# Decay totals of the chunks from the ninth on: a small DMA in place of one-column matmuls, with a new order

## The chip, the cores and the metric

The kernel runs on one core of a Trainium2 chip. The metric is the device time of one execution in microseconds; lower is better. Instructions stand in one queue for each engine (PE for matmuls, DVE, ACT, POOL), and SP issues the DMAs; each queue is worked off strictly in order, and engines wait for one another by semaphores.

## The reference

There are two layers, one after the other. The first is a linear attention with a state and a decay for each channel (batch 4, 8 heads, 768 tokens, 48 channels a head):

```python
for t in range(S):
    cur = np.einsum('bhd,bhe->bhde', u[None] * kt, vt)
    y[:, :, t] = np.einsum('bhd,bhde->bhe', rt, state + cur)
    state = wt[:, :, :, None] * state + np.einsum('bhd,bhe->bhde', kt, vt)
```

The second takes y as 3072 tokens of 384 features: `h = x @ w_in` (384 to 2048), `g = s * relu(h)**2 + b`, `out = g @ w_out` (2048 to 384). Inputs and output are fp32.

## The kernel before

**Chunks.** The attention is done in 24 chunks of 128 tokens of one batch row, all 8 heads at once, 384 columns. Chunks 0 to 3 are in pairs ("packed") and follow a way of their own. From chunk 8 on, chunk n and chunk n+4 belong to the same batch row, one after the other; the chunks 20 to 23 are the last of each row and leave no state. Two chunks of attention give one MLP tile of 256 tokens; there are 12 tiles.

**One chunk from 8 on.** ACT takes the logarithm of w (`ln`, L317). PE forms running sums of it over the chunk's tokens with a triangular matrix (`cum`, L391), and four more matmuls with a single column of ones give the total over all 128 tokens, with two heads' channels on the partitions (L397), in four extra columns of the same PSUM tile. ACT takes the exponential of the sums and of the totals in one instruction (`exp`, L413) into `E[:, 0]`; the total's exponential, `lam`, is the decay over the whole chunk. DVE forms the inclusive sum (`inc`, L418) and ACT its negative exponential into `E[:, 1]` (`exn`, L428). DVE multiplies r and k by both halves of E in one instruction (`mul`, L444) into `prd`. There are two buffers of E, used in turn by the chunks.

**State.** POOL spreads `lam` to `l2` (L458). PE forms the chunk's addition to the state (`dmm`, L638), DVE adds the old state (`sup`, L679), and POOL scales the sum by `l2` (`st`, L688). The new state is used by chunk n+4.

**Output of a chunk.** `prd` is transposed, on PE with a copy by ACT for chunks up to 8 (`tr` L471, `tev` L494), by a DMA transpose from chunk 9 on (L501). PE forms the token by token products (`mt`, L543), DVE masks them (`msk`, L555), PE sums over tokens and adds what the state gives (`ymm`, L597 and L606). POOL makes the part with u (`rkp` L322, `rku` L328, `yd` L351), with a reduction on DVE (`cd`, L345); DVE adds it (`yev`, L651), PE transposes and ACT copies to the tile's `xT` (`xtr` L699, `xev` L714).

**MLP tile.** Eight groups of six matmuls with w_in (`g1`, L749), each followed by relu on ACT (L762) and a square on ACT (L772) or DVE (L774); then eight groups of four matmuls with w_out (`g2`, L793), DVE's evacuation (`oev`, L804) and the store (L823). The weights come in four pieces each (`li`, `lo`, L719 and L729), cast by `ci` and `co`.

**Order.** The order is written out by hand in one text, ORDER, of some 1,300 words such as `exp8.0`, and each engine's queue holds its own words in that order; a letter after @ chooses the engine (A, D, P). A number with a plus sign puts in that many matmuls on zeros, to keep PE going at the start. The figures in `add(...)` were a planner's and have no effect on the order that is written out; the buffers' counts (`E=2`, `l2=5`) are real. The core of the part to be changed is

```python
nc.scalar.activation(out=c["E"][:, x, 0:w], in_=ps[:, 0:w], func=AF.Exp)
...
in1=c["E"][:, :, 0:HD].rearrange("t x (h d) -> t x h d", h=H),
```

Of the kernel before, what the change touches and what calls it, by code (L numbers as in the profile page):

```python
# [8 lines left out]
FP32 = mybir.dt.float32  # L9
# [15 lines left out]
PK = 4  # L25
PKD = 1.55
# [12 lines left out]
load0.0 ln0 load0.2 load0.1 ln1 +17 cum0.0 cum0.1 exp0.0 mul0.0 cum1.0 cum1.1 exp0.1 exp1.0 mul0.1  # L39
+3 tr0 load0.3 l21 exp1.1 mul1.0 mul1.1 vb0@A l20 vb1@A load_u u_mm rkp0 tr1 dmm0 u_ev load2.0  # L40
load4.0 tev0 tev1 sup0 ln2 rku0 load2.1 st0 cd0 rkp1 ln3 +5 mt0 +1 cum2.0 cum2.1 load2.3 load2.2
msk0.0 li0 cum3.0 ln4 vb3@A msk1.0 exp2.0 vb2@A msk0.1 li2 +1 cum4.0 exp3.0 msk1.1 yd0 mul2.0 cum3.1
rku1 exp2.1 exp3.1 mul2.1 cd1 l22 mul3.0 ymm0 ci0@A ymm1 li1 yev0 exp4.0 tr2 dmm1 yd1 mul3.1 +8 xtr0
rkp3 li3 tev2 yev1 rku3 sup1 xev0 st1 tr3 rkp2 ci2@D xtr1 xev1 dmm2 sup2 lo0 tev3 load5.0 +3 g10.0
ci1@A mt2 msk3.0 relu0.0 lo1 g10.1 g10.2 msk2.0 msk2.1 sq0.0@A relu0.1 msk3.1 rku2 ci3@A g10.3 g10.4
st2 relu0.4 relu0.2 l23 l24 ymm3 cd3 sq0.1@D yd3 ymm2 lo2 cd2 lo3 yev3 xtr3 small2 yd2 co0@D g10.5
relu0.3 sq0.2@A sq0.4@A ln5 yev2 relu0.5 g10.6 xtr2 g20.4 xev2 csred0@D xev3 load6.0 load4.1 load4.2
load5.1 sq0.3@A load5.2 relu0.6 cum5.0 g10.7 co1@D sq0.5@A load6.1 csred1@D csadd1@D co2@D g11.0
g20.0 relu0.7 exp5.0 sq0.7@A relu1.0 g11.1 csred2@D cum5.1 exp5.1 sq0.6@A g20.1 g11.2 g11.3 cum4.1
g20.5 co3@D small relu1.3 relu1.2 relu1.1 sq1.0@A load7.0 csadd2@D load6.2 ln6 load4.3 load5.3 g20.6  # L50
g11.4 csred3@D g11.5 relu1.4 g20.2 exp4.1 csadd3@D load6.3 sq1.3@A g20.3 cum6.0 relu1.5 g20.7
cssplit sq1.1@A mul4 csspread sq1.2@D csevac g11.6 exp6.0 relu1.6 cum6.1 mul5 tr4 dmm3 exp6.1 l26
g11.7 tev4 tr5 oev0.1 tev5 sup3 relu1.7 sq1.4@A oev0.0 g21.0 g21.1 rkp4 mt4 rkp5 g21.4 vb4@P mul6
msk5.0 sq1.5@A sq1.7@A rku4 rku5 msk4.0 load8.0 l25 msk4.1 tr6 cd4 dmm4 load9.0 sup4 yd4 load7.1 st4
load7.2 sq1.6@A vb5@A cd5 ln7 vb6@A tev6 load7.3 msk5.1 load8.1 ln8 g21.5 g21.2 g21.6 load8.2 dmm5
cum7.0 exp7.0 yd5 ymm4 g21.7 sup5 yev4 ymm5 cum7.1 xtr4 cum8.0 yev5 inc8 load9.3 load10.0 load9.1
ln9 dmm6 rkp6 st3 l27 exp7.1 load11.0 load8.3 xev4 vb7@P xtr5 xev5 cum9.0 exp8.0 mul7 load9.2 sup6
g21.3 exn8 g12.0 exp9.0 g12.1 rkp7 rku6 relu2.0 tr7 g12.2 relu2.1 inc9 st5 oev1.1 oev1.0 sq2.1@A
rku7 g12.3 dmm7 tev7 relu2.2 sq2.0@D relu2.3 g12.4 sup7 mul8 cd6 rkp8 relu2.4 g12.5 g22.4 mt6
relu2.5 g22.0 msk6.0 sq2.3@A tr8 g12.6 msk7.0 msk6.1 cd7 sq2.2@A sq2.5@A msk7.1 g22.5 ymm6 ln10  # L60
g22.1 yd6 rku8 sq2.4@A yev6 tev8 exn9 cd8 relu2.6 ln11 yd7 vb8@P st7 ymm7 xtr6 g22.6 cum10.0 yev7
xev6 store0.1 load11.1 vb9@A mul9 inc10 xtr7 l29 l28 rkp9 g12.7 load10.1 xev7 cum11.0 g22.2 g13.0
st6 relu2.7 exp10.0 dmm9 sq2.7@D load11.2 g13.1 store0.0 load10.2 exn10 g13.2 exp11.0 inc11 sq2.6@A
relu3.0 sq3.0@A exn11 sup9 relu3.1 mul10 rku9 dmm8 g13.3 sup8 mul11 tev9 g22.7 g13.4 g13.5 load11.3
load10.3 load12.0 load13.0 g22.3 oev2.1 cd9 tev11 load12.1 tev10 oev2.0 relu3.3 relu3.2 st8 rkp10
relu3.4 mt8 l211 yd9 msk8.0 msk8.1 g13.6 sq3.1@A sq3.4@A relu3.5 sq3.3@A l210 yd8 g23.4 rku10 vb10@A
g13.7 relu3.7 vb11@P msk9.0 sq3.2@A rkp11 ymm8 msk9.1 g23.0 ln12 yev8 st9 ymm9 xtr8 relu3.6 g23.1
sq3.6@A sq3.5@D yev9 cum12.0 xev8 xtr9 xev9 inc12 store1.0 ln13 exp12.0 dmm11 g23.5 load12.2 sup11
g23.2 dmm10 cd10 g14.0 sup10 exn12 relu4.0 rku11 load13.3 mt10 g23.6 g14.1 sq3.7@A msk10.0 msk10.1
msk11.0 cum13.0 g14.2 g14.3 store1.1 load13.1 msk11.1 inc13 mul12 cd11 load13.2 load14.0 relu4.1  # L70
ymm10 relu4.2 sq4.0@D exp13.0 rkp12 store2.1 relu4.3 exn13 g23.3 g23.7 yd10 load16.0 load15.0
load14.1 sq4.1@A ymm11 g14.4 load14.3 oev3.1 yd11 rkp13 g24.0 g14.5 st11 rku12 g14.6 load14.2
sq4.2@A sq4.3@A ln14 relu4.4 load15.1 l212 relu4.5 mul13 relu4.6 yev11 load12.3 oev3.0 yev10 rku13
xtr11 g24.4 ln15 sq4.5@A xtr10 cum14.0 vb13@P sq4.4@D g14.7 inc14 xev10 g24.1 g24.5 l213 xev11 cd13
exp14.0 cum15.0 g15.0 exn14 relu4.7 g15.1 load15.2 relu5.0 cd12 inc15 relu5.1 exp15.0 tev12 exn15
sq4.6@A sq5.1@D mul14 sq4.7@D g15.2 g24.2 g24.6 g15.3 l215 ln16 tev13 relu5.3 store2.0 sq5.0@D g15.4
g24.3 vb14@P vb12@A relu5.2 l214 yd12 mul15 cum16.0 dmm13 g15.5 inc16 load17.0 sq5.3@A dmm12
load15.3 tev14 relu5.5 oev4.0 exp16.0 relu5.4 tev15 st10 sq5.2@A g24.7 g25.4 sup13 l216 rkp15 st13
g15.6 sq5.4@A mt12 store3.0 load16.1 yd13 sq5.5@A rku15 store3.1 relu5.6 sup12 oev4.1 ln17 g15.7
msk12.0 load18.0 vb15@A load16.2 g25.5 dmm14 exn16 relu5.7 g25.0 msk13.0 rkp14 msk12.1 cum17.0 ymm12  # L80
msk13.1 exp17.0 sq5.7@A g25.1 ymm13 load17.1 load16.3 yev12 sup14 xtr12 yev13 xev12 load17.2 dmm15
inc17 g25.6 xtr13 rku14 load17.3 st12 sq5.6@A sup15 cd15 g25.2 mt14 load18.1 load19.0 msk14.0
msk15.0 exn17 g25.7 xev13 msk14.1 g16.0 cd14 g16.1 yd15 yd14 g16.2 msk15.1 rkp16 relu6.0 sq6.0@A
relu6.2 relu6.1 ymm14 g16.3 ymm15 yev14 g16.4 xtr14 yev15 relu6.3 sq6.3@A sq6.1@A g16.5 oev5.1 mul16
xtr15 st14 sq6.2@A g16.6 xev14 g26.4 l217 g25.3 g16.7 tev16 relu6.4 load18.2 rkp17 xev15 vb16@P
relu6.5 g17.0 g26.5 relu6.6 relu6.7 sq6.5@A rku16 st15 vb17@P rku17 mul17 sq6.4@D oev5.0 ln18 g17.1
dmm16 relu7.1 cum18.0 sq6.6@D sq6.7@A inc18 sup16 cd17 relu7.0 sq7.0@D g17.2 tev17 cd16 relu7.2
load18.3 store4.0 load20.0 store4.1 load19.1 exp18.0 ln19 g26.0 g26.1 g17.3 dmm17 g26.2 g17.4
cum19.0 yd17 load21.0 l218 vb18@P load19.2 yd16 load20.1 st16 exn18 sq7.1@A relu7.3 g26.6 sup17
inc19 relu7.4 sq7.3@A exp19.0 sq7.4@A mt16 g17.5 msk16.0 msk17.0 msk17.1 g17.6 g26.3 g26.7 ln20  # L90
relu7.5 msk16.1 ymm17 exn19 sq7.5@A oev6.1 sq7.2@A g17.7 relu7.6 relu7.7 yev17 sq7.6@A ymm16 g27.4
load19.3 store5.1 l219 rkp18 ln21 g27.5 rku18 load22.0 load20.2 cum20.0 xtr17 yev16 xtr16 oev6.0
# [71 lines left out]
def kernel(  # L164
# [72 lines left out]
    NBX = 4  # L237
    PRD_B = 4
    MB = 4
    NLW = 3  # L240
    logws = [
        const.tile([128, H, 64], BF16, name=f"logw{i}", tag=f"logw{i}")
        for i in range(NLW)
# [916 lines left out]
```

## Time and profile before

| what | us |
|---|---|
| median of three runs | 184.68 (184.1 to 184.84) |
| the profiled execution | 184.8 |
| its span, first to last instruction | 183.0 |
| PE busy | 176.2 |
| ACT busy | 145.4 |
| DVE busy | 143.9 |
| POOL busy | 104.4 |
| one product L444, mean of 20 | 1.228 |
| one activation L413 / L428, mean | 0.498 / 0.529 |
| one one-column matmul L397, mean of 64 | 0.164 |

The profile's page gives busy time by engine, then the span in 40 slices of 4.6 us with the busy tenths of each engine, then the chain of work that ended last, then groups of instructions with the idle time of the engine before them. Means of groups on PE are latencies of pipelined matmuls: two that follow one another start closer than the mean says. Line numbers are those of the kernel before.

### The profile page before, as it was taken

To read this page: it belongs to the slowest core of one execution; us is meant where nothing else is said; L and a number is where in the kernel's file an instruction comes from. 1 tells how busy PE (TensorE), PEld (TensorE's weight loads), DVE (VectorE), ACT (ScalarE), POOL (GpSimd) and SP (SyncE) were. 2 spreads that over 40 slices of the span, in tenths; PEclk is the share of its full clock that TensorE was granted. 3 is DMA by queue.
4 is the path that set the end of the run, shared out by engine and by line. 5 is a ranking of instruction groups with operands and counts; after the bars stand their busy time and mean duration, and the time that the engine had idled before them with its cause. 6 is when DMAs were issued, how large, how long until landed. Compare 5 with 4: busy or idle time off the path is not lost.

```text
span 183.0 us, 5106 instructions
## 1 busy us (share of the span) xinstructions
PE 176.2 (96%) x1994; PEld 139.8 (76%) x1994; DVE 143.9 (79%) x251; ACT 145.4 (79%) x285; POOL 104.4 (57%) x139
## 2 busy tenths in 40 slices
PE   7999699999999999999999999999999999999992
PEld 5568588777798798687887798877876798788871
DVE  7587599999999989899589889768779897670432
ACT  3875999999999998969899869997897395685530
POOL 3695950008997869828478769778508694130000
PEclk9999999999999999999999999999999999999999
DMA  5999999979979689998999973999599919810112
GB/s 153 313 277 337 386 387 358 179 144 212 201 150 230 137 171 147 235 217 163 211 201 178 231 154 61 197 206 225 106 207 197 223 23 161 217 61 31 43 43 86
DMA packets 113449, 34.14 MB, mean 187 GB/s; under 512 B 108177, under 2 KB 111378, under 8 KB 113426
## 3 DMA queue, kind: packets, MB, share of 16 engines
q1 hardware_dynamic: 113426, 33.83, 81.2%
q8 instruction: 15, 0.25, 0.5%
q14 instruction: 8, 0.07, 0.1%
HBM read 25.17 MB, written 4.72 MB: 163 GB/s over the span
## 4 chain that ended last, share of the span: by engine, by line
PE 83%; SPq 6%; DMA 5%; DVE 2%; ACT 1%; issue 1%; DVEq 0%
PE o_ps L793 34%; PE h_ps L749 33%; DMA wi_st<-in_moe_w_in_dram 5%; SPq L304 4%; PE mt_ps L543 3%; PE y_ps L606 2%; PE xt_ps L699 2%; PE cums L391 2%; PE y_ps L597 2%; PE d_ps L638 2%; SPq L719 1%; PE trps L471 1%; DVE prd L444 1%; ACT w_in L870 1%; PE y_ps L586 1%
## 5 line engine op out<-in xcount | busy, mean ns | idle before, releaser
L749 PE MATMUL h_ps<-xT,w_in 128*128 128x256 bf16 x576 | 72.9, 273 | 1.5 <-ACT xT L714 1.3
L793 PE MATMUL o_ps<-w_out,gT 128*128 128x384 bf16 (+1 forms) x400 | 73.0, 319 | 0.1
L762 ACT ACTIVATE rh<-h_ps 128x512 bf16<-128x512 f32 x96 | 54.8, 601 | 14.8 <-PE h_ps L749 14.2
L749 PEld LDWEIGHTS <-w_in 128*128 128x128 bf16 x576 | 61.2, 114 | 5.9 <-issue 1.4
L793 PEld LDWEIGHTS <-gT 128*128 128x128 bf16 x400 | 36.5, 98 | 17.1 <-issue 0.2
L772 ACT ACTIVATE gT<-rh 128x512 bf16<-128x512 bf16 x68 | 41.4, 639 | 0.3
L351 POOL TENSOR_TENSOR yd<-vt,cd 128x384 bf16<-128x384 f32 x20 | 17.7, 887 | 24.0 <-DVE cd L345 17.4
L555 DVE TENSOR_TENSOR mt_sb<-mt_ps,tri_strict 128x512 bf16<-128x512 f32 x40 | 25.0, 681 | 2.3 <-PE mt_ps L543 2.2
L328 POOL TENSOR_TENSOR rku<-rkp,u_bc 128x384 f32<-128x384 f32 x24 | 25.4, 1064 | 0.6
L774 DVE TENSOR_TENSOR gT<-rh 128x512 bf16<-128x512 bf16 x28 | 15.7, 574 | 12.4 <-ACT rh L762 12.3
L444 DVE TENSOR_TENSOR prd<-rkt,E 128x768 bf16<-128x768 f32 x20 | 24.5, 1228 | 0.0
L322 POOL TENSOR_TENSOR rkp<-rkt 128x384 f32<-128x384 f32 x20 | 21.1, 1058 | 1.9 <-DMA rkt<-in_k_dram 1.9
L413 ACT ACTIVATE E<-cums 128x388 f32<-128x388 f32 (+1 forms) x32 | 15.6, 498 | 3.6 <-PE cums L391 1.9
L804 DVE SCALAR_TENSOR_TENSOR o_sb<-o_ps,s_bc,bconst 128x384 f32<-128x384 f32 (+1 forms) x25 | 14.7, 594 | 4.5 <-PE o_ps L793 4.4
L688 POOL TENSOR_TENSOR st<-stmp,l 128x384 bf16<-128x384 bf16 x16 | 17.1, 1072 | 1.8 <-DVE stmp L679 1.8
L458 POOL TENSOR_TENSOR l<-E,par 128x8 f32<-128x8 f32 x20 | 6.5, 330 | 20.2 <-ACT E L413 20.2
L651 DVE TENSOR_TENSOR x_sb<-y_ps,yd 128x384 bf16<-128x384 f32 x24 | 13.3, 553 | 3.9 <-PE y_ps L606 3.1
L714 ACT COPY xT<-xt_ps 128x384 bf16<-128x384 bf16 x24 | 11.0, 487 | 3.1 <-PE xt_ps L699 3.1
L345 DVE TENSOR_REDUCE cd<-rku 128x8 f32<-128x384 f32 x24 | 13.0, 544 | 0.2
L418 DVE TENSOR_TENSOR inc<-cums,logw 128x384 f32<-128x384 f32 x16 | 8.8, 552 | 3.9 <-PE cums L397 1.4
L317 ACT ACTIVATE logw<-wt 128x384 bf16<-128x384 f32 x20 | 10.6, 529 | 0.0
L679 DVE TENSOR_TENSOR stmp<-d_ps,st 128x384 bf16<-128x384 f32 x16 | 8.7, 549 | 1.5 <-PE d_ps L638 1.3
(93 smaller groups left out, 202.0 us busy)
## 6 DMA issues: line engine op xcount, KB each, us to landing
out_dram<-o_sb SPq DMA_DIRECT2D x23, 192.0 KB, 3.1
wt<-in_w_dram SPq DMA_DIRECT2D x20, 192.0 KB, 3.9
rkt<-in_r_dram SPq DMA_DIRECT2D x20, 192.0 KB, 3.9
rkt<-in_k_dram SPq DMA_DIRECT2D x20, 192.0 KB, 4.0
vt<-in_v_dram SPq DMA_DIRECT2D x20, 192.0 KB, 3.8
wi_st<-in_moe_w_in_dram SPq DMA_DIRECT2D x4, 768.0 KB, 7.4
wo_st<-in_moe_w_out_dram SPq DMA_DIRECT2D x4, 768.0 KB, 7.0
pkt<-in_w_dram SPq DMA_DIRECT2D x2, 384.0 KB, 3.7
```

The lines of the kernel that those rows point to most:

```text
L322: nc.gpsimd.tensor_tensor(out=rkp, in0=c["r"], in1=c["k"], op=ALU.mult)
L328: nc.gpsimd.tensor_tensor(out=rku.rearrange("t h d -> t (h d)"), in0=c["rkp"].rearrange("t h d -> t (h d)"), in1=u_bc, op=ALU.mult,)
L351: nc.gpsimd.tensor_tensor(out=yd, in0=c["v"], in1=c["cd"].unsqueeze(2).to_broadcast([128, H, D]), op=ALU.mult,)
L413: nc.scalar.activation(out=c["E"][:, x, 0:w], in_=ps[:, 0:w], func=AF.Exp)
L444: nc.vector.tensor_tensor(out=prd[:, :, :, 0:D], in0=c["rk"], in1=c["E"][:, :, 0:HD].rearrange("t x (h d) -> t x h d", h=H), op=ALU.mult,)
L555: nc.vector.tensor_tensor(out=c["mt"][:, sg], in0=c["mt_ps"][sg], in1=(masks[:, n % 2] if packed(n) else tri_strict) .unsqueeze(1) .to_bro ...
L688: nc.gpsimd.tensor_tensor(out=c["st_new"], in0=c["stmp"].rearrange("q p (g e) -> q p g e", g=2), in1=c["l2"].unsqueeze(3).to_broadcast([12 ...
L749: nc.tensor.matmul(ps[:, f, :], lhsT=w_in_sb[ft // FPP][:, kt, :].rearrange("p (m j) -> p j m", j=FPP)[:, ft % FPP, :], rhs=xT[T][:, kt, : ...
L762: nc.scalar.activation(out=rh, in_=hs[T, i], func=AF.Relu)
L772: nc.scalar.activation(out=g, in_=rh, func=AF.Square)
L774: nc.vector.tensor_tensor(out=g, in0=rh, in1=rh, op=ALU.mult)
L793: nc.tensor.matmul(os_[T, k][:, cols], lhsT=gT[T][:, ft, tt * 128 : (tt + 1) * 128], rhs=w_out_sb[ft // FPP][:, ft % FPP, cols], start=(ft ...
```

## The change

From chunk 8 on (`LAM = 8`), PE no longer forms the total. The negative exponential of the inclusive sum at the chunk's last token, row 127 of `E[:, 1]`, is 1 over the same decay. Two DMAs (`lam`, by SP) carry this one row to the partitions of the state, one for the even and one for the odd heads, 48 partitions of 4 values each, into a ring of six small tiles. DVE then takes the reciprocal of 128x4 and spreads it to `l2` (128x8), which POOL did before. Chunks 20 to 23 need no total and had none.

So that the row can be carried, E of these chunks is stored with the channel outside and the head inside ("d h" in place of "h d"). Both activations write it so, and the product reads it so: neighbours along the inner loop of 48 lie 8 words apart. Buffer E is released by the product and by the two DMAs, in place of POOL's L458. `dmm` and `sup` no longer wait for `l2`.

The copies `tev` and `xev` can now be put on ACT or DVE, and the whole ORDER is another one: over all, 6 copies `xev` and 3 `tev` are on DVE, 23 squares in place of 28, and the first pieces of w_in are asked for earlier. The matmuls on zeros at the start are 21 of 512 columns, where they were 38 of 256.

```diff
--- before.py
+++ after.py
@@ constants @@
 PK = 4
+LAM = 8
...
 ORDER = """
-load0.0 ln0 load0.2 load0.1 ln1 +17 cum0.0 cum0.1 exp0.0 mul0.0 cum1.0 cum1.1 exp0.1 exp1.0 mul0.1
-+3 tr0 load0.3 l21 exp1.1 mul1.0 mul1.1 vb0@A l20 vb1@A load_u u_mm rkp0 tr1 dmm0 u_ev load2.0
...
+load0.0 load_u ln0 load0.1 load0.2 +6 u_mm ln1 load2.0 cum0.0 cum0.1 exp0.0 load0.3 exp0.1 cum1.0
+cum1.1 exp1.0 mul0.0 mul0.1 exp1.1 ln2 mul1.0 +1 tr0 mul1.1 u_ev ln3 l21 +2 tr1 li0 tev0@D cum2.0
...
+load9.2 g21.7 load11.0 dmm6 xev5@D load10.1 lam8 rkp6 tr7 oev1.0 store0.1 dmm7 g12.0 sup6 oev1.1
...
+lam10 tev10 lam11 g13.7 msk8.1 msk9.1 ymm8 oev2.0 vb10@A cd9 relu3.6 cum12.0 exp12.0 rku10 ymm9 yd9
...
 """
@@ -238,6 +240,7 @@
     PRD_B = 4
     MB = 4
     NLW = 3
+    lams = const.tile([128, 6, 8], FP32, name="rlam", tag="rlam")
     logws = [
         const.tile([128, H, 64], BF16, name=f"logw{i}", tag=f"logw{i}")
         for i in range(NLW)
@@ -392,7 +395,7 @@
             ps[:, 0:HD], lhsT=tri_strict if x == 0 else ntri_incl,
             rhs=lw[:, :, 0:D], start=True, stop=True,
         )
-        if x == 0 and cc < NCH - 1:
+        if x == 0 and cc < NCH - 1 and not row_lam(n):
             for p in range(HP):
                 nc.tensor.matmul(
                     ps[:, HD + p : HD + p + 1],
@@ -402,6 +405,12 @@
                     stop=(p == HP - 1),
                 )
 
+    def by_head(ap, n):
+
+        if row_lam(n):
+            return ap.rearrange("t (d h) -> t h d", h=H)
+        return ap.rearrange("t (h d) -> t h d", h=H)
+
     def expo(n, x):
         c = cb[n]
         cc, _ = coords(n)
@@ -409,8 +418,12 @@
         if x == 0:
             E = work.tile([128, 2, HD + 16], FP32, name="E", tag="E", bufs=2)
             c["E"], c["lam"] = E, E[:, 0, HD : HD + HP]
-        w = HD + HP if x == 0 and cc < NCH - 1 else HD
-        nc.scalar.activation(out=c["E"][:, x, 0:w], in_=ps[:, 0:w], func=AF.Exp)
+        w = HD + HP if x == 0 and cc < NCH - 1 and not row_lam(n) else HD
+        if row_lam(n):
+            out, in_ = by_head(c["E"][:, x, 0:HD], n), by_head(ps[:, 0:HD], 0)
+        else:
+            out, in_ = c["E"][:, x, 0:w], ps[:, 0:w]
+        nc.scalar.activation(out=out, in_=in_, func=AF.Exp)
 
     def incl(n):
         c = cb[n]
@@ -426,7 +439,7 @@
     def expn(n):
         c = cb[n]
         nc.scalar.activation(
-            out=c["E"][:, 1, 0:HD], in_=c["inc"], func=AF.Exp, scale=-1.0
+            out=by_head(c["E"][:, 1, 0:HD], n), in_=by_head(c["inc"], 0), func=AF.Exp, scale=-1.0
         )
 
     def mult(n, x=None):
@@ -444,9 +457,22 @@
         nc.vector.tensor_tensor(
             out=prd[:, :, :, 0:D],
             in0=c["rk"],
-            in1=c["E"][:, :, 0:HD].rearrange("t x (h d) -> t x h d", h=H),
+            in1=c["E"][:, :, 0:HD].rearrange(
+                "t x (d h) -> t x h d" if row_lam(n) else "t x (h d) -> t x h d", h=H
+            ),
             op=ALU.mult,
         )
+
+    def row_lam(n):
+        return n >= LAM
+
+    def lamrow(n):
+        c = cb[n]
+        t = lams[:, n % 6]
+        row = c["E"][127:128, 1, 0:HD].rearrange("o (d p g) -> o d p g", g=2, p=HP)
+        for g in range(2):
+            nc.sync.dma_start(out=t[64 * g : 64 * g + D, 0:HP], in_=row[:, :, :, g])
+        c["rlam"] = t
 
     def lam2(n):
         c = cb[n]
@@ -455,6 +481,17 @@
             return
         l2 = work.tile([128, 32], FP32, name="l2", tag="l2", bufs=5)[:, 0 : 2 * HP]
         l2 = l2.rearrange("q (p g) -> q p g", g=2)
+        if row_lam(n):
+            t = c["rlam"]
+            nc.vector.reciprocal(out=t[:, HP : 2 * HP], in_=t[:, 0:HP])
+            nc.vector.tensor_tensor(
+                out=l2,
+                in0=t[:, HP : 2 * HP].unsqueeze(2).to_broadcast([128, HP, 2]),
+                in1=par.unsqueeze(1).to_broadcast([128, HP, 2]),
+                op=ALU.mult,
+            )
+            c["l2"] = l2
+            return
         nc.gpsimd.tensor_tensor(
             out=l2,
             in0=c["lam"].unsqueeze(2).to_broadcast([128, HP, 2]),
@@ -480,6 +517,12 @@
                 )
         c["trps"] = ps
 
+    def move(name, out, in_):
+        if pl.ops[name]["eng"] == "ACT":
+            nc.scalar.copy(out=out, in_=in_)
+        else:
+            nc.vector.tensor_copy(out=out, in_=in_)
+
     def tevac(n):
         c = cb[n]
         if packed(n):
@@ -488,10 +531,10 @@
                 pair["RK2"] = work.tile(
                     [128, 2, 2 * HP, 128], BF16, name="RK2", tag="RK2", bufs=1
                 )
-            nc.scalar.copy(out=pair["RK2"][:, n % 2], in_=c["trps"])
+            move(("tev", n), pair["RK2"][:, n % 2], c["trps"])
             return
         RK = work.tile([128, 2 * HP, 128], BF16, name="RK", tag="RK", bufs=RKB)
-        nc.scalar.copy(out=RK, in_=c["trps"])
+        move(("tev", n), RK, c["trps"])
         c["RT"] = RK[:, 0:HP, :]
         c["KT"] = RK[:, HP : 2 * HP, :]
 
@@ -666,8 +709,8 @@
             [128, HP, 2 * D], BF16, name=f"st{bb}", tag=f"st{bb}", bufs=2
         )
         new_v = new.rearrange("q p (g e) -> q p g e", g=2)
-        lbc = c["l2"].unsqueeze(3).to_broadcast([128, HP, 2, D])
         if cc == 0:
+            lbc = c["l2"].unsqueeze(3).to_broadcast([128, HP, 2, D])
             nc.vector.tensor_tensor(
                 out=new_v,
                 in0=c["d_ps"].rearrange("q p (g e) -> q p g e", g=2),
@@ -711,7 +754,7 @@
         T, j = divmod(n, CPT)
         if j == 0:
             xT[T] = mlp.tile([128, KT, TOK], BF16, name="xT", tag="xT", bufs=XTB)
-        nc.scalar.copy(out=xT[T][:, :, j * L : (j + 1) * L], in_=c["xt_ps"])
+        move(("xev", n), xT[T][:, :, j * L : (j + 1) * L], c["xt_ps"])
 
 
     def load_win(i):
@@ -858,7 +901,7 @@
     pl = Plan(
         dict(w=WB, rk=8, v=VB, lw=NLW, prd=NPR, E=2, RK=RKB, M=MB, vb=6, yd=6, x=XSB, RK2=1,
              cd=4, rkp=2, rku=2, l2=5, P=6, o=2, gT=3, xT=XTB, rh=4, inc=1,
-             o_sb=4, wst=4, stmp=2)
+             o_sb=4, wst=4, stmp=2, rlam=6)
     )
     add = pl.add
 
@@ -934,11 +977,11 @@
             [("yd", [("yev", n)])], P - 1, port=True)
         for x in range(1 if one else 2):
             add(("cum", n, x), "PE",
-                (0.35 if pk else 0.163) + (0 if x or not keep else 0.21 if pk else 0.105),
+                (0.35 if pk else 0.163) + (0 if x or not keep or row_lam(n) else 0.21 if pk else 0.105),
                 cum, (n, x), every("ln"),
                 [("P", [("exp", n, x)] + ([("inc", n)] if one else []))], P, lat=0.2, slack=SL)
             add(("exp", n, x), "ACT", 0.43, expo, (n, x), [("cum", n, x)],
-                [] if x else [("E", muls(n) + ([("l2", n)] if keep else []))], P - 3,
+                [] if x else [("E", muls(n) + ([("lam" if row_lam(n) else "l2", n)] if keep else []))], P - 3,
                 after=[("exp", n, 0)] if x else [])
         if one:
             add(("inc", n), "DVE", 0.48, incl, (n,), [("cum", n, 0)], [("inc", [("exn", n)])], P - 3)
@@ -983,11 +1026,15 @@
             add(("xev", n), "SP", 1.2, dxtr, (n,), [("yev", n)] + xd, xt,
                 P - 1000, dma=0.85, slack=0.1)
         if keep:
-            add(("l2", n), "POOL", 0.17, lam2, (n,), [("exp", n, 0)],
+            if row_lam(n):
+                add(("lam", n), "SP", 0.9, lamrow, (n,), [("exn", n) if one else ("exp", n, 1)],
+                    [("rlam", [("l2", n)])], P - 2, dma=0.25)
+            add(("l2", n), "DVE" if row_lam(n) else "POOL", 0.2 if row_lam(n) else 0.17, lam2, (n,),
+                [("lam", n)] if row_lam(n) else [("exp", n, 0)],
                 [("l2", [("st", n)])], P - 2, port=True)
-            add(("dmm", n), "PE", 0.36 if pk else 0.16, dmm, (n,), [a for m in b2 for a in muls(m)] + every("vb") + [("l2", n)] + prev,
+            add(("dmm", n), "PE", 0.36 if pk else 0.16, dmm, (n,), [a for m in b2 for a in muls(m)] + every("vb") + ([] if row_lam(n) else [("l2", n)]) + prev,
                 [("P", [("sup", n)])], P - 4, lat=0.2, slack=SL)
-            add(("sup", n), "DVE", 0.48, supd, (n,), [("dmm", n), ("l2", n)] + prev,
+            add(("sup", n), "DVE", 0.48, supd, (n,), [("dmm", n)] + ([] if row_lam(n) and cc else [("l2", n)]) + prev,
                 [("stmp", [("st", n)])] if cc else [], P - 5)
             if cc:
                 add(("st", n), "POOL", 0.8, sscale, (n,), [("sup", n), ("l2", n)]
@@ -1075,7 +1122,7 @@
         add(("co", i), e, t, cast_out, (i,), [("lo", i)], [], 45.0, port=e != "ACT")
 
 
-    warm_sb = const.tile([128, TOK], BF16, name="warm_sb", tag="warm_sb")
+    warm_sb = const.tile([128, 2 * TOK], BF16, name="warm_sb", tag="warm_sb")
     nc.vector.memset(warm_sb, 0.0)
     nc.vector.memset(logws[0], 0.0)
     make_upper_triangular(nc, tri_strict, val=1.0, diag=False)
@@ -1087,6 +1134,7 @@
     nc.vector.memset(par[0:64, 0:1], 1.0)
     nc.vector.memset(par[64:128, 1:2], 1.0)
     nc.vector.memset(prds[0], 0.0)
+    nc.gpsimd.memset(lams, 1.0)
     nc.vector.memset(logws[1], 0.0)
     for i in range(1, NPR):
         nc.vector.memset(prds[i], 0.0)
@@ -1112,7 +1160,7 @@
                 nc.gpsimd.tensor_copy(out=masks[d, i, c : c + 64], in_=src[d, d])
 
 
-    warm_ps = psO.tile([128, TOK], FP32, name="warm_ps", tag="o")
+    warm_ps = psO.tile([128, 2 * TOK], FP32, name="warm_ps", tag="o")
 
     def warm(n):
         for _ in range(n):
```

## The prediction

> **What bounds the kernel now.** I read the busy shares first, then the slices, then the chain:
>
> ```profile
> PE 176.2 (96%) x1994; PEld 139.8 (76%) x1994; DVE 143.9 (79%) x251; ACT 145.4 (79%) x285; POOL 104.4 (57%) x139
> ...
> PE   7999699999999999999999999999999999999992
> ...
> DVE  7587599999999989899589889768779897670432
> ACT  3875999999999998969899869997897395685530
> ...
> PE 83%; SPq 6%; DMA 5%; DVE 2%; ACT 1%; issue 1%; DVEq 0%
> ```
>
> PE is the bound: 96% busy, nines from the sixth slice to the last but one, 83% of the chain (the shares of SP and DMA are the first 24 us). But the rows of DVE and ACT are full of eights and nines, so PE leads by little. How little, a view of busy time by stretches says (stretch, length, then busy us and counts of PE, PEld, DVE, ACT, POOL, then granted clock, DMA share, GB/s):
>
> ```profile
> 56.00:152.00 96.00, 95.63 (x1058) 76.92 (x1057) 82.37 (x133) 82.06 (x169) 68.91 (x84) 1.00 0.89 177
> 24.00:56.00 32.00, 32.00 (x383) 26.05 (x381) 30.53 (x50) 31.11 (x61) 15.66 (x19) 1.00 0.96 227
> ```
>
> The first stretch holds the products L444 of chunks 8 to 23. DVE is free there for 96 - 82.37 = 13.6 us. In the second, DVE is 30.53 / 32 = 95.4% busy and PE never idles; I take 95.4% as what DVE can carry before PE starves, so 91.6 us of the 96, and the stage can take 91.6 - 82.4 = 9.2 us more DVE work. The groups and the PE timeline that the change touches:
>
> ```profile
> L444 DVE TENSOR_TENSOR prd<-rkt,E x20: 945/1178/1799, 40.0 to 150.7; 128x768 bf16<-128x768 f32 x20
> ```
> ```profile
> L444 DVE TENSOR_TENSOR prd<-rkt,E 128x768 bf16<-128x768 f32 x20 | 24.5, 1228 | 0.0
> L413 ACT ACTIVATE E<-cums 128x388 f32<-128x388 f32 (+1 forms) x32 | 15.6, 498 | 3.6 <-PE cums L391 1.9
> L458 POOL TENSOR_TENSOR l<-E,par 128x8 f32<-128x8 f32 x20 | 6.5, 330 | 20.2 <-ACT E L413 20.2
> ```
> ```profile
> 95.31 0.24 PE L397 MATMUL cums<-ones,logw 128*128 128x1 bf16 x4
> 95.41 0.33 PE L638 MATMUL d_ps<-vb,prd 128*128 128x96 bf16 x4
> ```
>
> The first line gives shortest, median and longest ns; the group lines give us in total, mean ns, and idle time before. The last pair shows what four one-column matmuls really take: each lasts 164 ns in its group (0.24 us for the four), but the next work starts 0.10 us after them.
>
> **What the Trainium skill says.** *Vector Engine (DVE) Microarchitecture Reference*, section 5.2 "Measured stream behaviour on trn2": a DVE port streams at full rate only in runs of at least two adjacent 4-byte words. It prices 1.054 ns per column when all is contiguous, 1.73 when one source hops at every element, 2.50 when both sources or the destination alone step 24 words. The trace agrees on the first: the shortest L444 is 945 ns, 768 x 1.054 = 809 plus 136 fixed. No instruction of the kernel before shows the others. *SBUF — State Buffer*, section "Who interferes with whom": a DVE instruction with two SBUF inputs contends with POOL's reads. L444 agrees: its mean of 1228 ns lies 283 above its shortest. *ScalarE: Activation LUTs*, section "What ACT_TABLE_LOAD costs": 186 + 0.833 N ns for an activation without pointer operands, so 506 for 384 columns; L413's mean is 498. *DMA: Bandwidth & Descriptors*, section "Rules for kernel authors": a strided last dimension is moved as one descriptor per element. No run here shows it yet.
>
> **The change part by part.**
>
> 1. *PE.* The decay column goes from 12 chunks (8 to 19), so 12 x 4 = 48 one-column matmuls at 0.10 us a group: -1.2 us of PE. All of it lies on the path while PE is the bound, none of it where another engine is.
>
> 2. *The layout of E.* This is what I count most. From chunk 8 on, E holds d outside and h inside, so both activations (L413, L428) write, and the product L444 reads, one fp32 every 8 words. L444 then has one source that never offers two adjacent words. Lower bound 768 x (1.73 - 1.054) = 0.52 us more each, upper bound 768 x (2.50 - 1.054) = 1.11, estimates from the section named. The section says small steps cost more than large ones; 8 words is small, but only one source steps. I take 0.8. For 16 products: 8.3, **12.8**, 17.8 us.
>
> 3. *Small DVE work added.* 12 reciprocals of 128x4 and 12 products of 128x8. The nearest rows are DVE's 128x2 memset (60 ns, L1086) and POOL's own 128x8 product (199 ns at its shortest, L458). At 0.12 us each: 24 x 0.12 = 2.9 us (1.4 to 4.8). POOL loses 12 x 0.33 = 4.0 us, off the path.
>
> 4. *Work moved between engines by the new order.* In tiles 2 to 9 DVE has 13 squares for 16: -3 x 0.574 = -1.7 us. Two copies of xT (chunks 11, 12) come to DVE: +1.0. Over the run, ACT has 73 squares for 68 (+5 x 0.64), 6 fewer copies of xT (-6 x 0.49), 3 fewer of RK (-3 x 1.02), 4 fewer casts of v (-4 x 0.52) and one more of w_in (+1.5): about -3.4 us. POOL takes 4 casts of v (+4 x 0.69) and one of w_out.
>
> 5. *ACT's strided writes.* No row and no page prices them. At nothing: 0. At double the column time: 0.833 x 384 = 0.32 us more for 32 activations, 10.2 us. With both in the stage ACT is at 82 + 10 = 92 of 96, below the 31.11 / 32 = 97% it carries from 24 to 56 us. So I count 0 on the path, 3 us at worst. A gain is excluded: nothing gets shorter.
>
> 6. *24 DMAs on SP.* The small b_bc load took 0.43 us to issue, so 24 x 0.43 = 10 us in a queue that waits 16.4 us for the product L444 alone (ahead of its transposes L501), with more behind stores. 192 elements each, 4,608 packets on top of 113,426: 4%. Each pair waits for L428 (or L413), and behind it in SP's order stand loads, stores and transposes. The transposes wait for L444, which itself waits for L428, so they lose only the issue. The landing (3.8 us for a transpose, the row of small consumers) stands before three things: the reciprocal on DVE, and behind it all DVE work in order; the scaling L688 on POOL, needed a whole round of four chunks later; and the reuse of E, two buffers, by the activation two chunks on, with the relus behind it on ACT. I take 0 here: in the new order the last two are mostly several us away. At worst, see the second rival.
>
> 7. *The head.* The first w_in piece is issued seventh instead of eleventh, the r, k and v of the second pair later; 38 warm matmuls of 256 columns become 21 of 512. In the trace the PE's last wait before dense work ends at 23.7 us, on a cast of w_in. Earlier weights against later v: I take 0, and 1.5 us either way.
>
> Sum for DVE in the stage: 82.4 + 12.8 + 2.9 - 1.7 + 1.0 = 97.4 us (92.9 to 102.4 with the two ends of part 2). It carries 91.6, so 5.8 us too much, and at 95.4% that takes 5.8 / 0.954 = 6.1 us (1.4 to 11.3). The saving on PE is lost, since PE then waits for masks, x and the squares from DVE. What is late next is PE at the first matmuls of an MLP tile and at the late squares. The profiled execution took 184.8 us for a span of 183.0; 184.8 + 6.1 = 190.9. The median of the three runs is 184.68, so the two stand alike.
>
> **The rivals.**
>
> *The stride is free, or fits into DVE's idle time: faster.* One mechanism: PE stays the bound and keeps the 1.2 us. 184.8 - 1.2 = 183.6, within 182.1 to 185.1 by the head. For it: below 9.2 us of added DVE work nothing should show, and the low end of part 2 with the other terms gives 82.4 + 8.3 + 2.2 = 92.9, only 1.3 over. It decides where the price of one product falls under (9.2 - 2.2) / 16 = 0.44 us. Against it: the section's price starts at 0.52.
>
> *The new transfers become the wait: slower, by another way.* The landing of 3.8 us, held by SP's order, keeps DVE at the reciprocal or ACT at the next E. Twelve transfers; if four come 2 us late on engines with 10% to spare, and PE's own queue of filled PSUM hides half: 4 us, 184.8 - 1.2 + 4 = 187.6. For it: both engines work strictly in order. Against it: in the new order DVE meets its reciprocal 3 to 20 us of PE work after the transfer. The sign would show in DVE idle before the reciprocal, not in longer products.
>
> *The change does not do what it says:* the instruction lists of the two built programs show 48 one-column matmuls and 24 more DMAs where the diff says so, so I leave no chance for it.
>
> **How the numbers follow.** The forecast, DVE over-full, 0.62; the stride hidden, 0.18; the transfers as the wait, 0.20. Half a per cent (0.9 us) is about what a measurement of this kernel can tell from no change. Faster: 0.13 of the second case, 0.01 of the third. Slower: 0.61, 0.01 and 0.17. Same: the rest, 0.07. The forecast alone spans 186.2 to 196.1, and ACT's 3 us could be on top; the range goes down to 184.0, to take in part of the hidden case, and up to 197.0.
>
> **What would show it.** Right: the products of chunks 8 to 23 last about 2.0 us in the mean (1.75 to 2.35), those before 1.2; DVE is at 95% or more from 56 to 152 us; PE shows waits for DVE (masks, x_sb, gT) of several us in sum where it had none. The one-column group has 16 matmuls left of 64. The activations that write E last between 0.50 and 0.82 us. Wrong: products still near 1.2 us, or PE as full as before in the stage. If the products are long and PE is still full, the 95.4% was too low a ceiling.

## The result and the profile after

The changed kernel takes **191.12 us** (median of four runs, 189.65 to 192.55), the kernel before 184.76 us on the same chip (four runs, 184.1 to 185.83). One of the four, 192.55 us, was in the slower state that some executions of any kernel show; such runs are left out of the ratio and of every median below, and the median of the other three is 190.75 us. The ratio is 1.031, 95% interval 1.022 to 1.040: slower, by 6.0 us between the medians. The profiled execution took 190.75 us, its span is 188.7 us.

The page's shares, the slices and the head of the chain, of the kernel after:

```profile
PE 178.4 (95%) x1929; PEld 137.0 (73%) x1929; DVE 156.4 (83%) x277; ACT 153.0 (81%) x278; POOL 112.0 (59%) x133
...
PE   6999798999999999999989999979989999999993
...
DVE  7379689999998999899799989689879897974322
ACT  3486697899989999989968897699699889863840
...
PE 43%; POOL 15%; DMA 11%; SPq 10%; issue 8%; DVE 7%; ACT 4%; POOLq 0%; ACTq 0%; DVEq 0%
```

PE still has 95% of the span, but its share of the chain falls from 83% to 43%. The row of PE has eights and sevens in the middle, where it had nines without a break. No other engine takes the bound over: POOL, DMA, SP, DVE and ACT share what PE lost. By stretches of the kernel after (stretch, length, busy us and counts of PE, PEld, DVE, ACT, POOL, then clock, DMA share, GB/s):

```profile
24.00:56.00 32.00, 30.89 (x377) 24.57 (x366) 30.76 (x48) 29.38 (x54) 18.03 (x22) 1.00 0.98 239
56.00:152.00 96.00, 93.14 (x971) 73.07 (x970) 86.45 (x150) 85.97 (x159) 70.01 (x69) 1.00 0.86 169
```

From 56 to 152 us PE is idle 2.9 us where it was idle 0.4, and from 24 to 56 us 1.1 us where it never idled. DVE is 86.45 / 96 = 90% busy in the later stretch, ACT as well: both fuller than before (82.4 and 82.1), neither full. The groups on the page of the kernel after that answer to those shown of before:

```profile
L457 DVE TENSOR_TENSOR prd<-rkt,E 128x768 bf16<-128x768 f32 x20 | 31.4, 1568 | 2.8 <-DMA rkt<-in_k_dram 1.9
...
L426 ACT ACTIVATE E<-cums 128x384 f32<-128x384 f32 (+1 forms) x32 | 21.8, 692 | 7.4 <-PE cums L383 2.1
...
L441 ACT ACTIVATE E<-inc 128x384 f32<-128x384 f32 x16 | 14.7, 919 | 0.1
```

The four early products and the other early activations are dense and pull the means of L457 and L426 down. The view of the single instructions shows the 16 products of chunks 8 to 23 at 1.66 us in the mean, 1.55 at the shortest (before: 1.25 and 0.945). The activations of these chunks take 0.89 us (L426, before 0.49) and 0.92 us (L441, before 0.53). So in this execution the written half of the layout costs each ACT instruction 0.39 us and the read half each product 0.42 us. The 0.39 stands in every kernel with strided writes below; the strided products of the others last longer, 1.71 to 1.81 us in the mean. The new transfers and the small DVE work, in the views by group and by DMA issue of the kernel after:

```profile
L487 DVE TENSOR_TENSOR l<-rlam,par 128x8 f32<-128x8 f32 x12 | 4.8, 401 | 0.4
L486 DVE RECIPROCAL rlam<-rlam 128x4 f32<-128x4 f32 x12 | 2.0, 166 | 0.0
```
```profile
rlam<-E SPq DMA_DIRECT2D x24, 0.8 KB, 2.6
```
```profile
POOL st L731 <- DVE l L487: 3.5, 2, 2.8
...
ACT E L426 <- DMA rlam<-E: 1.2, 2, 0.7
```

The second fence is the DMA's median from issue to landing, 2.6 us. The third is the view of waits (total us, times, longest): the state's scaling on POOL waits 3.5 us for a total, and an activation on ACT 1.2 us for the buffer that a transfer holds; neither engine is the bound.

### The profile page after: what moved, and what is told of

The parts are those of the page before. It is cut to its first block, busy times and chain, and to the rows that moved or that the text cites. A ratio compares the mean times of both kernels' runs of the same rounds, so it can differ in the third digit from the quotient of the medians.

```text
span 188.7 us, 5017 instructions
## 1 busy us (share of the span) xinstructions
PE 178.4 (95%) x1929; PEld 137.0 (73%) x1929; DVE 156.4 (83%) x277; ACT 153.0 (81%) x278; POOL 112.0 (59%) x133
## 4 chain that ended last, share of the span: by engine, by line
PE 43%; POOL 15%; DMA 11%; SPq 10%; issue 8%; DVE 7%; ACT 4%; POOLq 0%; ACTq 0%; DVEq 0%
PE h_ps L792 18%; PE o_ps L836 18%; SPq L307 4%; POOL rku L331 4%; DMA pkt<-in_v_dram 4%; POOL rkp L325 4%; POOL st L731 4%; DMA rlam<-E 3%; DMA wt<-in_w_dram 2%; DVE mt_sb L598 2%; ACT E L426 2%; DMA vt<-in_v_dram 2%; SPq L299 2%; DVE prd L457 2%; SPq L762 2%
## 5 line engine op out<-in xcount | busy, mean ns | idle before, releaser
L836 PE MATMUL o_ps<-w_out,gT 128*128 128x384 bf16 (+1 forms) x400 | 74.0, 320 | 0.8 <-ACT gT L815 0.6
L815 ACT ACTIVATE gT<-rh 128x512 bf16<-128x512 bf16 x73 | 44.3, 637 | 0.3
L457 DVE TENSOR_TENSOR prd<-rkt,E 128x768 bf16<-128x768 f32 x20 | 31.4, 1568 | 2.8 <-DMA rkt<-in_k_dram 1.9
L331 POOL TENSOR_TENSOR rku<-rkp,u_bc 128x384 f32<-128x384 f32 x24 | 27.6, 1152 | 1.8 <-DVE u_bc L940 1.0
L325 POOL TENSOR_TENSOR rkp<-rkt 128x384 f32<-128x384 f32 x20 | 25.6, 1284 | 4.9 <-DMA rkt<-in_k_dram 4.9
L426 ACT ACTIVATE E<-cums 128x384 f32<-128x384 f32 (+1 forms) x32 | 21.8, 692 | 7.4 <-PE cums L383 2.1
L817 DVE TENSOR_TENSOR gT<-rh 128x512 bf16<-128x512 bf16 x23 | 13.2, 587 | 6.0 <-ACT rh L805 5.9
L915 POOL CAST vb<-vt 128x384 bf16<-128x384 f32 x16 | 12.0, 756 | 5.5 <-DMA vt<-in_v_dram 5.4
L441 ACT ACTIVATE E<-inc 128x384 f32<-128x384 f32 x16 | 14.7, 919 | 0.1
L694 DVE TENSOR_TENSOR x_sb<-y_ps,yd 128x384 bf16<-128x384 f32 x24 | 12.8, 551 | 1.6 <-PE y_ps L649 1.0
L522 ACT COPY xT<-xt_ps 128x384 bf16<-128x384 bf16 x18 | 8.7, 494 | 4.8 <-PE xt_ps L742 4.8
```

What stands on the lines that cost most here:

```text
L325: nc.gpsimd.tensor_tensor(out=rkp, in0=c["r"], in1=c["k"], op=ALU.mult)
L331: nc.gpsimd.tensor_tensor(out=rku.rearrange("t h d -> t (h d)"), in0=c["rkp"].rearrange("t h d -> t (h d)"), in1=u_bc, op=ALU.mult,)
L426: nc.scalar.activation(out=out, in_=in_, func=AF.Exp)
L441: nc.scalar.activation(out=by_head(c["E"][:, 1, 0:HD], n), in_=by_head(c["inc"], 0), func=AF.Exp, scale=-1.0)
L457: nc.vector.tensor_tensor(out=prd[:, :, :, 0:D], in0=c["rk"], in1=c["E"][:, :, 0:HD].rearrange("t x (d h) -> t x h d" if row_lam(n) else " ...
L815: nc.scalar.activation(out=g, in_=rh, func=AF.Square)
```

## The experiments

All times are medians, set against runs of the kernel before on the same chip beside them; "+2.0" means over that. These were 184.32 us for experiments 1 to 4; 184.56 for the first two kernels of experiment 5, for experiment 6 and for the first kernel of experiment 7; 184.12 for the last two of experiment 5; and 185.13 for the last two of experiment 7. In experiments 1 to 3 and in the dense kernels of experiment 5 some products or totals take other channels' decays, as the expectations say; their time is read, not their output.

**1. The layout taken away.** The kernel after, with both activations and the product dense; order, DMAs and reciprocals stay.

```diff
     def by_head(ap, n):
-        if row_lam(n):
-            return ap.rearrange("t (d h) -> t h d", h=H)
         return ap.rearrange("t (h d) -> t h d", h=H)
...
-                "t x (d h) -> t x h d" if row_lam(n) else "t x (h d) -> t x h d", h=H
+                "t x (h d) -> t x h d", h=H
```

> The changed kernel, with E of every chunk stored with heads outside as before: both activations write and the product reads adjacent words. All else (order, DMAs, reciprocals) stays; the DMAs still pick the same addresses, so the decays they carry belong to other channels. Theory 1 (the one-word steps of E cost the time): products near 1.23 us and activations near 0.50 and 0.53 us, time 184 to 186.5 us. Theory 2 (the new order costs it) and theory 3 (waits for the new transfers cost it): 189 to 191 us although the instructions are short again.

Measured: 186.62 us, ratio 1.013 (1.008 to 1.018), +2.3. The stretches of this kernel:

```profile
24.00:56.00 32.00, 31.04 (x366) 24.78 (x365) 30.74 (x48) 29.06 (x55) 18.09 (x21) 1.00 1.00 239
56.00:152.00 96.00, 96.00 (x1032) 77.76 (x1031) 83.98 (x158) 81.96 (x167) 64.72 (x72) 1.00 0.90 180
```

The time lies just above the first range of the expectation. PE has no idle time left from 56 to 152 us; the idle time before 56 us stays. Of the 6.0 us, the layout is what is left, 6.0 - 2.3 = 3.7, and it acts in the stage of the later chunks.

**2 and 3. Each half of the layout alone.** First only ACT writes with steps and the product reads dense; then only the product reads with steps. Each is one of the two edits above undone.

> The changed kernel, but the product reads E as if heads were outside (adjacent words, so it multiplies by the decays of other channels); the activations still write one word in eight. Products 1.23 us, activations 0.89 and 0.92 us. If the cost is DVE's, as the prediction had it: 185 to 187 us. If ACT's longer writes carry it: 188 to 191 us.

> The changed kernel, but the activations write adjacent words and the product reads one word in eight (so it multiplies by the decays of other channels, and the DMAs carry those of other channels). Products 1.55 us at the shortest, activations 0.50 and 0.53. If the cost is DVE's: 188 to 191 us. If it is ACT's: 185 to 187 us.

Measured: ACT's half 188.26 us (ratio 1.019, 1.012 to 1.025), +1.6 over the dense kernel; DVE's half 188.65 us (1.023, 1.018 to 1.029), +2.0 over it. The groups and the later stretch, first of the kernel with ACT's half, then of that with DVE's:

```profile
L457 DVE TENSOR_TENSOR prd<-rkt,E 128x768 bf16<-128x768 f32 x20 | 22.7, 1133 | 3.0 <-ACT E L441 1.7 <-DMA rkt<-in_k_dram 1.2
...
L441 ACT ACTIVATE E<-inc 128x384 f32<-128x384 f32 x16 | 14.8, 923 | 0.0
```
```profile
56.00:152.00 96.00, 95.74 (x1013) 76.63 (x1011) 81.64 (x157) 89.20 (x164) 64.92 (x73) 1.00 0.86 172
```
```profile
L455 DVE TENSOR_TENSOR prd<-rkt,E 128x768 bf16<-128x768 f32 x20 | 33.4, 1671 | 0.6 <-DMA rkt<-in_k_dram 0.3 <-ACT E L424 0.2
...
L439 ACT ACTIVATE E<-inc 128x384 f32<-128x384 f32 x16 | 8.4, 525 | 0.5 <-DVE inc L429 0.4
```
```profile
56.00:152.00 96.00, 95.58 (x1004) 76.06 (x1002) 91.70 (x155) 80.18 (x162) 70.82 (x72) 1.00 0.83 169
```

Each half lengthens its own engine's instructions and not the other's activations or products. By the medians each costs time, about the same. For ACT's half that reading does not hold up. In its profiled execution the granted clock of PE fell to 0.72 in the mean from 31 to 37 us; the first activation that writes with steps starts only at 53.9 us. The same stretch, first in the dense kernel of experiment 1, then with ACT's half:

```profile
31.00:37.00 6.00, 5.44 (x47) 4.61 (x48) 5.93 (x10) 4.19 (x10) 0.00 (x0) 1.00 0.95 205
31.00:37.00 6.00, 5.09 (x30) 3.54 (x31) 5.93 (x11) 3.40 (x8) 0.00 (x0) 0.72 0.86 204
```

Three of the four runs with ACT's half had a mean granted clock of 0.988 or 0.989 and took 188.24 to 188.63 us. The fourth, at 1.000, took 186.47 us, which lies within the dense kernel's runs (185.18 to 187.38, all at 0.998 or more). So the times do not show that ACT's half alone costs anything. DVE's half took 187.87 to 188.69 us in its three runs at 0.998 or more: there the cost stands.

These kernels share one order, so their traces can be compared by work done: from the first w_in matmul of tile 2 to that of tile 10, read from PE's timeline (us). The drop of the clock lies before this stretch.

| kernel | tile 2 | tile 10 | between |
|---|---|---|---|
| dense (experiment 1) | 54.6 | 154.6 | 100.0 |
| ACT's half | 56.5 | 157.6 | 101.1 |
| DVE's half | 56.4 | 158.5 | 102.0 |
| both, the kernel after | 55.1 | 160.1 | 105.0 |

ACT's half costs 1.1 us here, DVE's 2.0, both together 5.0. These are single executions, so 1.1 us is an indication and no more. With DVE's half alone DVE is 91.70 / 96 = 95.5% busy and PE shows only 0.4 us of idle time from 56 to 152 us, yet 2.0 us are lost: the idle time of PE understates what it loses.

**4. The new order alone.** The kernel after with totals by matmul and a dense E everywhere; POOL spreads the total where the DMA stood in the order.

```diff
-LAM = 8
+LAM = 99
```

> The new order alone: the totals by one-column matmuls for every chunk again, E with heads outside, POOL spreads the decays at the places where the transfers stood; no new DMA, no reciprocal. Theory 1: 184.5 to 187 us. Theory 2 (order): 189 to 191 us. Theory 3 (transfers): 184.5 to 187 us, and then e1 should be slow where this one is fast.

Measured: 186.36 us, ratio 1.011 (1.007 to 1.014), +2.0. The stretches of this kernel:

```profile
24.00:56.00 32.00, 30.67 (x382) 24.41 (x371) 30.55 (x48) 28.87 (x55) 17.89 (x22) 1.00 1.02 251
56.00:152.00 96.00, 96.00 (x1062) 78.09 (x1061) 78.78 (x134) 81.12 (x164) 67.78 (x84) 1.00 0.89 179
```

The order costs 2.0 us without any new operation, and the time is lost before 56 us. Without those on zeros, the matmuls that PE has started by 56 us have 95,412 columns in this kernel and 102,712 in the kernel before. At this kernel's pace from 56 to 152 us, 96 / 225,068 = 0.427 ns a column, that is 3.1 us of work behind; at the end it is 2.2 us behind (spans 185.2 and 183.0).

Experiment 1 differs from this run by the swap of matmuls for DMAs, reciprocals and spreading: 186.62 against 186.36, with ranges that overlap (185.18 to 187.38 and 185.85 to 187.21). The times can't tell the two apart. In the traces, PE is busy 176.6 us there and 178.0 here, and from tile 2 to tile 10 it takes 100.0 us there and 101.0 here.

**5. The head of the kernel before in the new order.** The words up to the square of tile 1's fifth group are put back to before's, and the rest of the new order follows: once with a dense E, once on the whole change, once with the new order alone, and the first of them once more.

```diff
 ORDER = """
-load0.0 load_u ln0 load0.1 load0.2 +6 u_mm ln1 load2.0 cum0.0 cum0.1 exp0.0 load0.3 exp0.1 cum1.0
+load0.0 ln0 load0.2 load0.1 ln1 +17 cum0.0 cum0.1 exp0.0 mul0.0 cum1.0 cum1.1 exp0.1 exp1.0 mul0.1
...
```

> e1's kernel (changed kernel, E with heads outside, decays of other channels carried), but its order begins with the words of the kernel before up to sq1.4 (some 48 us, with its 256-column matmuls on zeros), and goes on with the new order's remaining words. If the new order's cost of about 2 us lies in the first 35 us, where PE idles: 183.0 to 184.6 us, PE on the first matmul of tile 1 at about 31 us. If it lies in the rest of the order: 185.5 to 187 us.

> The changed kernel whole, with E one word in eight and the right decays, but the head of the order of the kernel before as in e5. Additive parts: 191.1 less about 2.2, so 188 to 189.8 us. If the long products and the head wait for the same thing: still 190.5 to 191.5 us.

> The new order alone as before (totals by matmul, E dense), but its first 225 words, up to the square of tile 1's fifth group, are those of the kernel before. If the new order costs its 2 us in the head: 184.3 to 185.3, and PE reaches tile 1 at 31 us. If it costs them later, or if the cost is that of any splice of the two orders: 186 to 187.5.

> The dense kernel with the totals by DMA and the head of the kernel before once more, for its profile and beside the run before it. If the drop of the granted clock near 27 us in its first profile was chance and the head is what costs: about 185, without the drop. If not: 186.7 again.

Measured: dense 186.70 us (+2.1) and, repeated, 186.16 (ratio 1.010, 1.007 to 1.014, +2.0); the whole change 188.82 (1.021, 1.016 to 1.026, +4.3); the order alone 187.39 (1.015, 1.010 to 1.020, +3.3). The head helps the whole change by 1.7 us (+4.3 for +6.0), of which the traces put 1.5 us behind the head, from tile 2 to tile 10 (103.5 for 105.0); it helps the other two not at all. The +3.3 is in part the granted clock: four of the six runs had 0.979 to 0.991, the two at 1.000 took 186.20 and 186.22 us, which is +2.1. The early stretches of the order alone with the old head:

```profile
0.00:24.00 24.00, 20.23 (x265) 13.22 (x265) 16.62 (x40) 15.33 (x27) 15.75 (x33) 0.97 1.07 286
24.00:56.00 32.00, 31.21 (x388) 24.54 (x387) 29.24 (x48) 29.26 (x55) 14.26 (x21) 0.97 0.97 229
56.00:152.00 96.00, 96.00 (x1060) 78.15 (x1059) 78.58 (x135) 81.01 (x164) 67.74 (x84) 1.00 0.88 182
```

The idle time is still before 56 us, though the words there are largely before's; the granted clock is 0.97 in both early stretches of this execution, so part of the loss may be the clock's. From tile 2 to tile 10 the order alone takes 101.0 us again and the dense kernel (its first profile) 100.0, as with the new head, and the kernel before 102.1. So the order's cost lies before that stretch; which words of it cost stays open.

**6. The layout alone, in the order of the kernel before.** Totals by matmul, only E of chunks 8 to 23 with the channel outside; the total's exponential becomes an instruction of its own (12 of 128x4).

```diff
-        nc.scalar.activation(out=c["E"][:, x, 0:w], in_=ps[:, 0:w], func=AF.Exp)
+        nc.scalar.activation(
+            out=c["E"][:, x, 0:HD].rearrange("t (d h) -> t h d", h=H),
+            in_=ps[:, 0:HD].rearrange("t (h d) -> t h d", h=H),
...
+        if w > HD:
+            nc.scalar.activation(out=c["E"][:, x, HD:w], in_=ps[:, HD:w], func=AF.Exp)
```

> The kernel before in its own order, with totals by matmuls, and only E of chunks 8 to 23 stored one word in eight; the four columns of totals get an activation of their own in chunks 8 to 19 (12 short ones, some 0.2 us each). If the steps of E cost 4 to 5 us in any order: 188 to 190.5 us. If they cost only in the new order: 184.5 to 186.5 us.

Measured: 188.56 us, ratio 1.021 (1.015 to 1.027), +4.0. Its later stretch:

```profile
56.00:152.00 96.00, 93.97 (x1018) 73.86 (x1016) 83.48 (x129) 87.48 (x172) 73.83 (x82) 1.00 0.87 177
```

PE is idle 2.0 us in this stretch with DVE at 87% and ACT at 91%. From tile 2 to tile 10 this kernel takes 105.8 us, the kernel before 102.1: 3.7 us more. The layout costs about as much here as in the new order (3.7 in time), so its cost does not come from the order. With before's head on the new order the medians give less, 188.82 - 186.70 = 2.1, and the traces 3.5 from tile 2 to tile 10 (103.5 for 100.0); what makes the difference is not shown.

**7. The transfers without the new order.** Three kernels keep the order of the kernel before. Two keep E dense and let POOL copy the last 32 rows of E into the transfer's layout (one row buffer in the first, three in the second); the transfer stands right behind the exponential in the first, behind the chunk's copy or transpose of the products (or ahead of the next use of E's buffer) in the second. The third is the whole change, with its layout and no copy, and the later place.

```diff
-... exn12 relu4.0 ... tev12 exn15 ... st12 ...
+... exn12 lam12 relu4.0 ... tev12 exn15 ... st12 ...
```
```diff
-... exn12 relu4.0 ... tev12 exn15 ... st12 ...
+... exn12 relu4.0 ... lam12 exp14.0 ... tev12 exn15 ... l212 st12 ...
```

> The kernel before in its own order and with E as before, but decays of chunks 8 to 19 by DMA: POOL copies the last 32 rows of the negative exponential in the layout that the DMA needs, two DMAs follow each of L428, DVE takes reciprocal and product right after sup. Exact result. If dropping 48 one-column matmuls is worth its 1.2 us of PE and the transfers hide: 183.0 to 184.0 us. If the 12 copies on POOL or the transfers get in the way: 185 to 188 us.

> The order of the kernel before, E dense as before, the totals of chunks 8 to 19 by DMA as in the changed kernel, but with the transfer behind the chunk's copy or transpose of the products (or just ahead of the next use of its buffer of E, where that is earlier) and reciprocal and spreading just ahead of the state's scaling. POOL copies the last 32 rows of E to a row buffer in the transfer's layout (three buffers). If it was only the place in SP's queue that cost the earlier variant 20 us: 184.0 to 186.0, that is, the 1.2 us of PE minus little things. If transfers, reciprocals and the 12 copies of 0.9 us cost wherever they stand: 187 or more.

> The changed kernel whole (E strided, totals by DMA), but in the order of the kernel before, with the transfers placed late as in the run beside it. If the stride costs about 4 us and the new order about 2: 184.7 + 4 and up to 1.2 less, 187.4 to 188.9. If the new order was needed for the change to come out as well as it did (transfers fit badly into the old one): 191 or more.

Measured: 204.54 us (ratio 1.108, 1.102 to 1.114, +20.0), 201.85 (1.089, 1.083 to 1.094, +16.7) and 201.09 (1.084, 1.078 to 1.090, +16.0). The first lies outside both of its ranges; the other two fall under "187 or more" and "191 or more", 10 us and more above the figures named. In all three the granted clock is below 1 in some stretches; the two runs of the third at 0.999 and 1.000 still took 200.69 and 200.15 us. SP's own waits in the first of them, then engine waits, the group of the reciprocals and the later stretch of the third:

```profile
SPq L478 <- POOL u_row L472: 17.0, 6, 6.9
```
```profile
POOL st L731 <- DVE l L487: 16.2, 4, 6.4
...
ACT E L426 <- DMA rlam<-E: 7.6, 3, 2.9
```
```profile
L486 DVE RECIPROCAL rlam<-rlam 128x4 f32<-128x4 f32 x12 | 2.0, 170 | 0.0
```
```profile
56.00:152.00 96.00, 85.47 (x851) 65.88 (x850) 78.23 (x134) 80.33 (x150) 55.91 (x60) 0.98 0.81 161
```

In the first, SP stands 17 us at the transfer's issue, waiting for the copy; behind it stand loads and transposes. The third has no copy and a later place, and there POOL waits 16.2 us for the spread total (3.5 in the kernel after) and ACT 7.6 us for E to come free (1.2 in the kernel after). PE is idle 10.5 us of the stretch.

POOL's wait is not for the landing. In the third kernel every pair of transfers had landed 4.5 to 23.3 us before its reciprocal began, and DVE is never idle before a reciprocal. POOL waits because the second and third kernel place reciprocal and spreading one word ahead of the scaling (`l212 st12`), so DVE comes to them late; in the kernel after they stand 5 to 125 words ahead. ACT's wait is for the transfer itself, which stands late in SP's order.

The same layout with totals by matmul is at +4.0 in this order; with these transfers, reciprocals and spreading it is at +16.0. In the new order the same swap costs nothing that the times can tell. So the swap is cheap in the order that was written with it, and these places in the old order are dear. How much of the 12 us is the transfer's place and how much DVE's is not separated, and other places were not tried, so that none would do isn't shown.

## Why the prediction was right or wrong

The forecast of 190.9 us came out within 0.2 us of the median, and the layout of E was rightly named as the largest part. The sum reached the number with terms that were wrong in opposite directions, so that it came so close is luck.

1. *PE, -1.2 us.* The 48 matmuls are gone (16 of 64 are left), and PE is busy 1.4 us less in experiment 1 than in experiment 4. In these dense kernels, where PE never idles from 56 to 152 us, tile 2 to tile 10 takes 1.0 us less, in both pairs of traces. That it gains nothing where others hold PE up, as predicted for the whole change, no run isolates.

2. *The product, +0.8 us each, 12.8 in all: mis-sized.* The kernel after shows +0.42 in the mean, 16 x 0.42 = 6.7 us. The shortest grew by 0.60 us, (1.548 - 0.136) / 768 = 1.84 ns per column. Of the prices that were taken from the Trainium skill (*Vector Engine (DVE) Microarchitecture Reference*, section 5.2), the lower one, 1.73 ns for one source that hops at every element, was thus near; the midpoint was not. The mean grew by less than the shortest here, since it lay 0.30 us over the shortest before and 0.12 after; that is below the lower bound of the estimate, 0.52. With DVE's half alone the mean grew from 1.19 to 1.81 us, by 0.62, which is within it. Why the two differ stays open.

3. *Small DVE work at 0.12 us: mis-sized.* The reciprocal took 0.166 us and the spreading 0.40 in the mean: 6.8 us for 2.9.

4. *Moved work* went as listed: 23 squares on DVE for 28, 6 copies of xT and 3 of RK. Of the copies of xT three and not two fall into the stage (chunks 6, 11, 12), at 0.35 us each for the 0.5 taken, so their sum of 1.0 us stands. No run separates the moved work from the rest of the order.

5. *ACT's strided writes, 0 on the path: too low by the traces.* The bound of 0.32 us each (double the column time) was below the measured 0.39. The prediction compared ACT's sum, 92 of 96 us, with a ceiling of 97% and concluded that what fits costs nothing. With ACT's half alone ACT is at 89.2 of 96 us, under that ceiling, and tile 2 to tile 10 takes 1.1 us more; beside DVE's half the step to both is 105.0 - 102.0 = 3.0 us. The 3 us named as the worst case is not exceeded. The times of ACT's half alone do not show a cost, since its one run at full clock is as quick as the dense kernel.

6. *Transfers, 0 in the new order.* The size held: experiment 1 against 4 is +0.3 us, within what the runs can tell. They landed in 2.6 us for the 3.8 assumed, and brought 4,992 packets more for the 4,608 reckoned. The second rival priced late transfers at 4 us; in the old order the swap, as it was placed there, costs 16.0 - 4.0 = 12 us over the layout.

7. *The head, 0 with 1.5 us either way: too low.* The whole order costs 2.0 us, experiment 4, lost before 56 us.

*The ceiling of 95.4% as the mechanism did not hold.* The prediction said that DVE would be at 95% or more from 56 to 152 us and that PE would wait for its masks, x and squares. DVE is at 90%, and the prediction's own test ("DVE is at 95% or more") fails. So does the second: PE's longest named wait for DVE is 0.8 us, for x_sb. What the runs show in its place is the order 2.0 and the layout 3.7, with 0.3 for the swap that the times can't tell from nothing; the layout is the remainder in this sum, and experiment 6 gives it 4.0 on its own. Of its two halves DVE's is shown to cost time, ACT's only by the traces. That longer steps on the way from running sum to product (0.39 + 0.39 + 0.42 = 1.2 us per chunk) come out as late arrivals at PE, because two engines with little to spare work strictly in order, fits the spread-out chain after; it is argued, and no run isolates it.

The rivals: *stride free* falls, though the mean product (0.42) was under its point of decision (0.44); it decided by DVE's sum alone and left ACT out. *Transfers as the wait* falls for the change as made. Its sign, DVE idle before the reciprocal, shows in neither order; in the old one ACT waits 7.6 us for the transfers, and the longer wait is POOL's for the late reciprocal.

## What to carry to other kernels

A layout that suits one small transfer is paid for by every instruction that writes or reads the whole tile: here 192 values for each DMA against two activations and a product of 384 and 768 columns. Price both sides, and do not count added work at nothing because its engine stays below full: here the product's half alone lost 2.0 us of a stage with DVE at 95%, and both halves 5.0 with DVE and ACT at 90%. A new transfer, and the work that unpacks it, need their own place in every queue that they pass, and an order in which they are free is part of the change and has its own price; measure that order alone. And look at the granted clock of each run before a difference of 1 or 2 us is put down to an edit.

## What the runs showed of the hardware that was not expected

ACT took 1.7 to 1.8 times as long to write fp32 to SBUF at a step of 8 words: 384 columns took 0.89 us for 0.49 from PSUM and 0.92 for 0.53 from SBUF, so 0.39 / 384 = 1.0 ns more per column. *ScalarE: Activation LUTs*, section "What ACT_TABLE_LOAD costs", gives 0.833 ns per column; the dense activations agree, the strided ones do not. The DMA of 192 single values from one partition to 48 landed in 2.6 us, less than the 192 KB loads (3.7 us for v); SP took 0.60 us to issue one, where 0.43 had been taken.

A lower granted clock went with more time in the kernel before: over the experiments its 34 runs at a mean of 0.996 or more took 183.66 to 185.41 us, its 7 runs at 0.987 to 0.991 took 185.76 to 186.70. It is no fixed price: in the last run of experiment 5, five executions at 0.988 to 0.991 took 186.13 to 186.46 us, the two at 1.000 took 186.08 and 186.78.
